# Local attention and a state-space layer: 448 rows cut as 128, 128, 128 and 64, with the 64s of two tokens or steps side by side

## The chip, the cores and the metric

The kernel runs on one core of a Trainium2 chip. The metric is device time in microseconds (us), lower is better. The times of the kernel before are 172.17, 172.98 and 174.47 us, median 172.98. Engines are named as in the profile: PE is TensorE's matmul, PEld its weights load, DVE VectorE, ACT ScalarE, POOL GpSimd, SP SyncE, whose queue issues most transfers.

## The reference, cut to what matters

Two layers stand side by side; the output joins them along the last axis. S = 2048 tokens, D = 448.

```python
# A: sliding, dilated local attention, 16 heads of 28, window 8, dilation 2
qkv = (x @ wqkv).reshape(B, S, 3, H, Dh)
idx = pos[:, None] - 2 * arange(8)          # masked where negative
logits = einsum("bhsd,bhswd->bhsw", q, k[idx]) * Dh ** -0.5
o = einsum("bhsw,bhswd->bhsd", softmax(logits), v[idx])
a = o.reshape(B, S, D) @ wo
# B: diagonal complex state space layer with 448 states
h_t = Lam_bar * h_{t-1} + B_bar @ x_t       # over all 2048 steps
b = 2 * real(C @ h_t) + x * Dskip
out = concatenate([a, b], axis=-1)
```

## The kernel before, in words

All is bf16 with float32 sums. The queue of every engine is written out by hand: what the program says in one order is issued in that order. Only DVE's larger pieces wait in a list (`add`), and `pump` puts them out when the running total of DVE's costs is below that of PE's costs; `pe(...)`, `dve(...)` and `load[0] +=` keep these totals. They are costs written by the author, and they set DVE's order and not PE's.

The 2048 tokens lie on 128 partitions with 16 tokens (`j`) each. The 448 features, wherever they are contracted, are cut in four tiles of `KT` = 112 rows.

- `g_xta` (L299): for a pair of tokens, 8 transposes on PE (L304) and one copy on DVE (L305) give x with features on the rows.
- `proj(t, j)` (L309): q, k or v of one token: 4 matmuls 448 wide (L312), one ACT copy (L316). 48 of them.
- `b_weights` (L323), `b_x` (L332): the state space input weights (8 matmuls, L327), and x transposed for it (L337), copied by DVE for even and ACT for odd steps (L339, L342).
- `c_weights` (L345): 56 small transposes that put 64 columns each in the upper or lower half of a PSUM bank (L352).
- `ssm_in(hf, j)` (L365): for half `hf` of the states (four or three tiles of 128 rows, 64 states with real and imaginary part) and step `j` of 8: 4 matmuls 256 wide for each tile (L372), then, but for step 0, one with the step before (L378), then the ACT copies (L379). The 4 matmuls of a step stand ahead of those that need the step before.
- `scan_mul` (L384), `scan_pe` (L391), `scan_run` (L403), `scan_out` (L410): the recurrence over blocks of 8 steps, by turns on DVE and PE; `ssm_mix` (L415) brings its result to the steps.
- `ssm_out(j, cb)` (L428): the output: 7 matmuls with C (L432), 4 with the diagonal Dskip (L434), an ACT copy, a store.
- `logits`, `softmax` (L448, L481): all on DVE: eight products of 128 x 7168 (L457), sums of halves (L460, L463 and on), and the softmax.
- `pv_mul` (L517): attention times v on DVE (L520); `av(i)` (L526): the sum over the window, done on PE by matmuls with the identity (L537); `wo_j` (L550): the output projection of one token, 4 matmuls 448 wide (L554), a copy, a store.

The order of PE's work: transposes with the k and q projections; v with `b_x` and `b_weights` in between; the rest of q; `ssm_in` of the first half, `c_weights`, `ssm_in` of the second half with the scans in between; `ssm_mix` and `ssm_out`; then 40 steps of `av` with `wo_j` between them. PSUM has 8 banks, given out in turn (`bank`).

Of the kernel before, what the change touches and what calls it, by code (L numbers as in the profile page):

```python
# [14 lines left out]
J = 16  # L15
# [21 lines left out]
def kernel(  # L37
# [41 lines left out]
    BT = big.tile([KT, 4, NT, 128], BF16, tag="BT")  # L79
    xT = big.tile([KT, 4, T, NC], BF16, tag="xT")  # L80
# [3 lines left out]
    dgD = big.tile([KT, 4, KT], BF16, tag="dgD")  # L84
# [5 lines left out]
    wts = wbuf[0:KT].rearrange("p (a k n) -> p a k n", a=3, k=4)  # L90
# [3 lines left out]
    xTA = u3[0:KT].rearrange("p (k j n) -> p k j n", k=4, j=J)  # L94
# [3 lines left out]
    w_r = A_wqkv.rearrange("(k p) n -> p k n", p=KT)  # L98
    xB_r = B_x[0].rearrange("(c p j) d -> p c j d", p=128, j=T)

    def load_w(t):
        SP.dma_start(wts[:, t], w_r[:, :, t * D:(t + 1) * D])
# [6 lines left out]

    load_x(14, 16)  # L110
# [6 lines left out]
    prow = const.tile([3 * NT, 2, HS], BF16, tag="prow")  # L117
    for i, vec in enumerate((B_Lambda_re, B_Lambda_im, B_log_dt)):
        ACT.dma_start(prow[NT * i:NT * (i + 1)], vec.rearrange("(t i) -> t i", i=HS).unsqueeze(1).to_broadcast((NT, 2, HS)))
    drow = const.tile([4, KT], BF16, tag="drow")  # L120
    ACT.dma_start(drow[:], B_Dskip.rearrange("(t i) -> t i", i=KT))
# [76 lines left out]
    def sincos(sin_out, cos_out, y, tmp):  # L198
        V.tensor_scalar(tmp, y, 1.0, MAGIC, ALU.mult, ALU.add)
        V.scalar_tensor_tensor(tmp, tmp, -MAGIC, y, ALU.add, ALU.subtract)  # L200
        ACT.activation(sin_out, tmp, ACTF.Sin, scale=-2 * PI * SHR)
        ACT.activation(tmp, tmp, ACTF.Abs)
        ACT.activation(cos_out, tmp, ACTF.Sin, bias=hpib[:], scale=-2 * PI * SHR)

# [6 lines left out]
    prm = pt_("prm", (128, 3, NT))  # L211
    lre, lim, ld = prm[:, 0], prm[:, 1], prm[:, 2]
    dsk = pt_("dsk", (KT, 4))
# [8 lines left out]
    def params_in():  # L222
        tp = bank(BF16)
        PE.transpose(tp[:, 0:3 * NT], prow.rearrange("p a i -> p (a i)"), ident[0:3 * NT, 0:3 * NT])
        V.tensor_copy(prm.rearrange("p a b -> p (a b)"), tp[:, 0:3 * NT])
        tp = bank(BF16)
        PE.transpose(tp[0:KT, 0:4], drow[:], ident[0:4, 0:4])
        V.tensor_copy(dsk[:], tp[0:KT, 0:4])
        ACT.activation(dt[:], ld, ACTF.Exp)
        dve(0.3)  # L230

    def params1():
# [3 lines left out]
        ACT.activation(rk[:], rk[:], ACTF.Exp)  # L236
# [3 lines left out]
        sincos(sn[:], cs[:], yk[:], tk[:])  # L240
# [3 lines left out]
        V.reciprocal(den[:], den[:])  # L244

# [35 lines left out]
    def build_D():  # L281
        V.tensor_tensor(dgD[:], ident[0:KT, 0:KT].unsqueeze(1).to_broadcast((KT, 4, KT)),
                        dsk.unsqueeze(2).to_broadcast((KT, 4, KT)), ALU.mult)
# [14 lines left out]

    def g_xta(jp):  # L299
        tp = bank(BF16)  # L300
        tpv = tp[0:KT].rearrange("p (k j n) -> p k j n", k=4, j=2)
        for kt in range(4):
            for jj in range(2):
                PE.transpose(tpv[:, kt, jj, :], xnA[:, 2 * jp + jj, KT * kt:KT * (kt + 1)], ident[:])  # L304
        V.tensor_copy(xTA[:, :, 2 * jp:2 * jp + 2, :], tpv)  # L305
        dve(0.69)
        load[0] += 0.45

    def proj(t, j):  # L309
        ps = bank()  # L310
        for kt in range(4):
            PE.matmul(ps[:, 0:D], xTA[:, kt, j, :], wts[:, t, kt, :], start=(kt == 0), stop=(kt == 3))  # L312
        src = ps[:, 0:D].rearrange("p (h d) -> p d h", h=H)
        dst = (q_s[:, :, j * H:(j + 1) * H] if t == 0 else
               k_s[:, :, HALO + j, :] if t == 1 else v_s[:, HALO + j])
        ACT.copy(dst, src)  # L316
        count[2] += 1
        if acts and count[2] > 18 and count[2] % 2 == 0:
            acts.pop(0)()
        pe(0.76)  # L320


    def b_weights(t):  # L323
        ps = bank()
        for kt in range(4):
            for i in range(2):
                PE.matmul(ps[0:KT, 128 * kt:128 * (kt + 1)], Bn[:, t, KT * kt:KT * (kt + 1)], G[:, i, t, :],  # L327
                          start=(kt == 0 and i == 0), stop=(kt == 3 and i == 1))
        ACT.copy(BT[:, :, t, :], ps[0:KT].rearrange("p (k n) -> p k n", k=4))
        pe(0.45)  # L330

    def b_x(j):  # L332
        tp = bank(BF16)
        tpv = tp[0:KT].rearrange("p (k c n) -> p k c n", k=4, c=2)
        for kt in range(4):
            for c in range(2):
                PE.transpose(tpv[:, kt, c, :], xnB[:, c, j, KT * kt:KT * (kt + 1)], ident[:])  # L337
        if j % 2 == 0:
            V.tensor_copy(xT[:, :, j, :], tp[0:KT].rearrange("p (k n) -> p k n", k=4))  # L339
            dve(0.69)  # L340
        else:
            ACT.copy(xT[:, :, j, :], tp[0:KT].rearrange("p (k n) -> p k n", k=4))  # L342
        load[0] += 0.45

    def c_weights(t2):  # L345
        n = min(2, NT - 2 * t2)
        tp = bank(BF16)
        for i in range(n):
            t = 2 * t2 + i
            for ri in range(2):  # L350
                for dt_ in range(4):
# [13 lines left out]
    def ssm_in(hf, j):  # L365
        banks = []
        for pr_ in pairs(halves[hf]):
            ps = bank()
# [157 lines left out]
    def av(i):  # L526
# [3 lines left out]
        if s == 0:  # L530
            accs[n_] = [bank() for _ in range(nj)]
# [175 lines left out]
```

## Time and profile before

| | us |
|---|---|
| median of 3 runs | 172.98 |
| the profiled execution's own time | 172.66 |
| its span | 170.9 |
| PE busy (95% of the span) | 162.5 |
| DVE busy (86%) | 146.7 |
| ACT busy (56%) | 95.7 |
| PE idle from 33 to 71 us | 0.00 |
| PE idle from 71 to 75.6 us | 1.56 |
| PE idle from 98.3 to 126.7 us | 0.00 |
| PE idle from 126.7 to 167.5 us | 0.01 |

The granted TensorE clock is 0.998 over the execution. Busy time counts an engine as busy while at least one instruction is in it. Matmuls overlap in PE, so the mean duration of one is longer than the time that it adds to a run of its kind; that time is read from the starts of the runs in the timeline. A line as `L312 PE MATMUL b<-wbuf,u 112*128 112x448 bf16 x192` says: L312 is line 312 of the listing; PSUM bank `b` is written from the weights `wbuf` and the data `u`; the weights are 112 rows by 128 columns, the streamed data 112 rows by 448, and there are 192 of them. A timeline row has start, duration from the first start to the last end, engine, line, operation and, in square brackets, how long the engine was idle ahead of it and what released it.

### The profile page before, as it was taken

To read this page: it belongs to the slowest core of one execution; us is meant where nothing else is said; L and a number is where in the kernel's file an instruction comes from. 1 tells how busy PE (TensorE), PEld (TensorE's weight loads), DVE (VectorE), ACT (ScalarE), POOL (GpSimd) and SP (SyncE) were. 2 spreads that over 40 slices of the span, in tenths; PEclk is the share of its full clock that TensorE was granted. 3 is DMA by queue.
4 is the path that set the end of the run, shared out by engine and by line. 5 is a ranking of instruction groups with operands and counts; after the bars stand their busy time and mean duration, and the time that the engine had idled before them with its cause. 6 is when DMAs were issued, how large, how long until landed. Compare 5 with 4: busy or idle time off the path is not lost.

```text
span 170.9 us, 3793 instructions
## 1 busy us (share of the span) xinstructions
PE 162.5 (95%) x1584; PEld 120.0 (70%) x1586; DVE 146.7 (86%) x179; ACT 95.7 (56%) x184; POOL 2.8 (2%) x22
## 2 busy tenths in 40 slices
PE   6799999999999999959999899999999999999992
PEld 6565655777756888838886555655679988888870
DVE  1399999899999999999998999989999999656811
ACT  3095569999887355524469954496430527145431
POOL 3000000000000000000010000000000000000000
PEclk9999999999999999999999999999999999999999
DMA  5999990892099000000000002202232010111112
GB/s 164 319 244 208 351 216 22 183 162 37 4 188 186 2 4 0 4 0 0 0 4 0 0 27 70 68 28 80 76 106 80 0 58 30 58 54 56 58 54 81
DMA packets 13279, 14.01 MB, mean 82 GB/s; under 512 B 4543, under 2 KB 12495, under 8 KB 13135
## 3 DMA queue, kind: packets, MB, share of 16 engines
q1 hardware_dynamic: 13191, 13.77, 32.1%
q8 instruction: 12, 0.20, 0.5%
q14 instruction: 5, 0.04, 0.1%
q10 hardware_dynamic: 71, 0.01, 0.0%
HBM read 6.89 MB, written 3.67 MB: 62 GB/s over the span
## 4 chain that ended last, share of the span: by engine, by line
PE 50%; DVE 34%; ACT 6%; issue 4%; DMA 3%; SPq 0%; DVEq 0%; ACTq 0%
PE b L537 17%; PE b L432 12%; DVE u L457 11%; PE b L554 7%; PE b L312 6%; DVE u L460 6%; DVE l L463 3%; DMA u<-in_A_x_dram 3%; PE b L422 2%; PE b L420 2%; DVE R L207 2%; PE b L434 2%; DVE l L466 2%; ACT k_s L316 2%; DVE u L406 1%
## 5 line engine op out<-in xcount | busy, mean ns | idle before, releaser
L312 PE MATMUL b<-wbuf,u 112*128 112x448 bf16 x192 | 40.1, 352 | 0.1
L520 DVE TENSOR_TENSOR k_s<-u,v_s 128x1792 bf16<-128x1792 bf16 (+1 forms) x40 | 33.8, 903 | 6.2 <-PE b L537 6.2
L537 PEld LDWEIGHTS <-k_s 128*112 128x112 bf16 x512 | 30.6, 130 | 2.0
L457 DVE TENSOR_TENSOR u<-q_s,k_s 128x7168 bf16<-128x7168 bf16 x8 | 31.1, 3889 | 0.9 <-ACT tab L294 0.5
L537 PE MATMUL b<-ident,k_s 128*112 128x128 bf16 x512 | 30.9, 219 | 0.0
L312 PEld LDWEIGHTS <-u 112*128 112x128 bf16 x192 | 17.7, 97 | 14.0 <-DVE u L305 0.5
L372 PE MATMUL b<-xT,BT 112*128 112x256 bf16 x224 | 26.9, 272 | 0.1
L379 ACT CAST u<-b 128x512 bf16<-128x512 f32 (+1 forms) x32 | 15.6, 535 | 19.0 <-PE b L378 16.7
L372 PEld LDWEIGHTS <-BT 112*128 112x128 bf16 x224 | 21.7, 97 | 3.3
L432 PE MATMUL b<-Cw,u 128*128 128x448 bf16 x112 | 23.8, 352 | 0.0
L559 ACT CAST ya<-b 128x448 bf16<-128x448 f32 x15 | 8.1, 537 | 16.8 <-PE b L554 13.4
L460 DVE TENSOR_TENSOR u<-u 128x3584 bf16<-128x3584 bf16 x8 | 16.2, 2022 | 0.1
L432 PEld LDWEIGHTS <-u 128*128 128x128 bf16 x112 | 10.5, 98 | 7.5
L436 ACT CAST yo<-b 128x448 bf16<-128x448 f32 x16 | 8.4, 534 | 12.1 <-PE b L434 8.7
L554 PE MATMUL b<-u,q_s 112*128 112x448 bf16 x64 | 14.4, 352 | 0.0
L423 ACT CAST u<-b 128x512 bf16<-128x512 f32 (+1 forms) x28 | 13.1, 561 | 0.4 <-PE b L422 0.4
L547 ACT CAST q_s<-b 112x512 bf16<-112x512 f32 x14 | 7.3, 595 | 8.1 <-PE b L537 8.0
L316 ACT CAST q_s<-b 128x448 bf16<-128x448 f32 x16 | 8.5, 532 | 4.3 <-PE b L312 4.3
L316 ACT CAST k_s<-b 128x448 bf16<-128x448 f32 x16 | 8.0, 533 | 4.2 <-PE b L312 4.2
L422 PE MATMUL b<-u,R 128*128 128x255 bf16 x49 | 9.5, 272 | 0.7 <-ACT u L413 0.7
L420 PE MATMUL b<-u,ident 128*128 128x512 bf16 (+1 forms) x28 | 9.9, 353 | 0.0
L316 ACT CAST v_s<-b 128x448 bf16<-128x448 f32 x16 | 9.2, 612 | 0.8 <-PE b L312 0.8
(119 smaller groups left out, 179.7 us busy)
## 6 DMA issues: line engine op xcount, KB each, us to landing
u<-in_B_x_dram SPq DMA_DIRECT2D x2, 896.0 KB, 14.4
out_dram<-yo SPq DMA_DIRECT2D x16, 112.0 KB, 1.7
out_dram<-ya SPq DMA_DIRECT2D x16, 112.0 KB, 1.7
u<-in_A_x_dram SPq DMA_DIRECT2D x3, 448.0 KB
wbuf<-in_A_wqkv_dram SPq DMA_DIRECT2D x3, 392.0 KB, 7.4
k_s<-k_s SPq DMA_DIRECT2D x1, 784.0 KB
v_s<-v_s SPq DMA_DIRECT2D x1, 784.0 KB, 5.9
k_s<-k_s SPq DMA_DIRECT2D x1, 588.0 KB, 10.6
```

What stands on the lines that cost most here:

```text
L312: PE.matmul(ps[:, 0:D], xTA[:, kt, j, :], wts[:, t, kt, :], start=(kt == 0), stop=(kt == 3))
L316: ACT.copy(dst, src)
L372: PE.matmul(ps[:, i * NC:(i + 1) * NC], BT[:, kt, t, :], xT[:, kt, j, :], start=(kt == 0 and i == 0), stop=(kt == 3 and j == 0 and i == le ...
L379: ACT.copy(Z[:, pr_[0]:pr_[0] + n, j, :], ps[:, 0:n * NC].rearrange("p (t c) -> p t c", t=n))
L420: PE.matmul(ps[:, 0:n * NC], ident[:], Z[:, sl, j, :], start=True, stop=False)
L423: ACT.copy(Z[:, sl, j, :], ps[:, 0:n * NC].rearrange("p (t c) -> p t c", t=n))
L432: PE.matmul(ps[:, 0:D], Z[:, t, j, cols], Cw[:, t, :], start=(t == 0), stop=False)
L457: V.tensor_tensor(pr[:], qv, kv, ALU.mult)
L460: V.tensor_tensor(pr[:, :, 0:14, :], pr[:, :, 0:14, :], pr[:, :, 14:28, :], ALU.add)
L520: V.tensor_tensor(pv_of(i), attn[:, s, H * j0:H * (j0 + nj)].rearrange("p (j h) -> p j h", h=H) .unsqueeze(2).to_broadcast((128, nj, DH, H ...
L537: PE.matmul(acc[kt // kb][0:KT, o:o + 128], pvf[:, jj, KT * kt:KT * (kt + 1)], ident[:], start=(s == 0 and o == 0), stop=(s == W - 1 and o ...
L554: PE.matmul(ps[:, 0:D], oTs[n_ % 3][:, kt, jj, :], wo_p[:, kt, :], start=(kt == 0), stop=(kt == 3))
```

## The change

Wherever 448 rows are contracted, the four tiles of 112 become three of 128 and a rest of 64. Two rests, of two tokens or two steps, lie on rows 0 to 63 and 64 to 127 of the same tile, and their products are issued one after the other, each on its half of the array's rows and into a bank of its own (`pair_product`, `sums_half`). Where a 64 wide result is transposed or summed, two go to columns 0 to 63 and 64 to 127 of the array and to the two halves of a bank's partitions (`transposes`, `b_weights`, `av`). For that, projections and output projection work on pairs of tokens, and `ssm_in` becomes a generator that puts the input sums of two steps out ahead of the steps that use them. `ssm_out` has three products 128 wide and one 64 wide, alone on half of the rows, for the skip.

Moved along with it: the weights' last 64 rows are loaded twice, once for each half of the partitions, by transfers of their own (two on ACT's queue at the start, two on SP's); the parameters gain Dskip, and are transposed after the first projection pair; the exponent and the sines of the parameters get a place of their own (`params_act`); `c_weights` goes to and fro between the halves; one logits buffer gets memory of its own; `oTs` has two buffers where it had three; DVE's list is pumped at a few more places, and the first `scan_mul` comes after five of DVE's eight logits products where it came after six.

```diff
-    xT = big.tile([KT, 4, T, NC], BF16, tag="xT")
+    xT = big.tile([128, T // 2, 7, NC], BF16, tag="xT")
...
     def load_w(t):
-        SP.dma_start(wts[:, t], w_r[:, :, t * D:(t + 1) * D])
+        SP.dma_start(wts[:, t, 0:3], w_r[:, :, t * D:(t + 1) * D])
+
+    def load_wh(eng, ts):
+        for i in range(2):
+            eng.dma_start(wts[HS * i:HS * (i + 1), ts, 3], wh_r[:, ts])
...
+    load_wh(ACT, slice(1, 2))
+    prow = const.tile([4 * NT, 2, HS], BF16, tag="prow")
+    for i, vec in enumerate((B_Lambda_re, B_Lambda_im, B_log_dt, B_Dskip)):
+        ACT.dma_start(prow[NT * i:NT * (i + 1)], vec.rearrange("(t i) -> t i", i=HS).unsqueeze(1).to_broadcast((NT, 2, HS)))
     load_x(14, 16)
     load_w(1)
...
+    load_wh(SP, slice(0, 3, 2))
     load_w(2)
...
+    def transposes(tp, x_of):
+        for kt in range(3):
+            for jj in range(2):
+                PE.transpose(tp[:, (2 * kt + jj) * 128:(2 * kt + jj + 1) * 128], x_of(jj, 128 * kt, 128 * (kt + 1)), ident[:])
+        for jj in range(2):
+            PE.transpose(tp[HS * jj:HS * (jj + 1), 768:896], x_of(jj, 384, 448), ident[:])
...
-    def proj(t, j):
-        ps = bank()
-        for kt in range(4):
-            PE.matmul(ps[:, 0:D], xTA[:, kt, j, :], wts[:, t, kt, :], start=(kt == 0), stop=(kt == 3))
+    def pair_product(lhs_of, rhs_of, rhs_half):
+        ps = [bank(), bank()]
+        for jj in range(2):
+            for kt in range(3):
+                PE.matmul(ps[jj][:, 0:D], lhs_of(jj, kt), rhs_of(kt), start=(kt == 0), stop=False)
+        for jj in range(2):
+            rows = slice(HS * jj, HS * (jj + 1))
+            PE.matmul(ps[jj][:, 0:D], lhs_of(jj, 3), rhs_half[rows], start=False, stop=True)
+        return ps
+
+    def proj(t, jp):
+        def lhs(jj, kt):
+            return xTA[:, jp, 2 * kt + jj, :] if kt < 3 else xTA[HS * jj:HS * (jj + 1), jp, 6, :]
+        ps2 = pair_product(lhs, lambda kt: wts[:, t, kt, :], wts[:, t, 3, :])
+        for jj in (1, 0):
...
+            ACT.copy(dst, src)
...
     def b_weights(t):
         ps = bank()
-        for kt in range(4):
+        for kt in range(3):
             for i in range(2):
-                PE.matmul(ps[0:KT, 128 * kt:128 * (kt + 1)], Bn[:, t, KT * kt:KT * (kt + 1)], G[:, i, t, :],
-                          start=(kt == 0 and i == 0), stop=(kt == 3 and i == 1))
+                PE.matmul(ps[:, 128 * kt:128 * (kt + 1)], Bn[:, t, 128 * kt:128 * (kt + 1)], G[:, i, t, :],
+                          start=(kt == 0 and i == 0), stop=False)
+        for i in range(2):
+            for a in range(2):
+                PE.matmul(ps[HS * a:HS * (a + 1), 384:512], Bn[:, t, 384:448], G[:, i, t, :],
+                          start=False, stop=(i == 1))
...
+    def b_x(jp, c):
         tp = bank(BF16)
+        transposes(tp, lambda jj, lo, hi: xnB[:, c, 2 * jp + jj, lo:hi])
+        o = xT[:, jp, :, 128 * c:128 * (c + 1)]
+        src = tp[:, 0:896].rearrange("p (k n) -> p k n", k=7)
+        if c == 0:
+            V.tensor_copy(o, src)
...
+            ACT.copy(o, src)
...
+    def sums_full(hf, j):
+        sums[hf, j] = [(bank(), pr_) for pr_ in pairs(halves[hf])]
+        jp, jj = j // 2, j % 2
+        for ps, pr_ in sums[hf, j]:
             for i, t in enumerate(pr_):
+                for kt in range(3):
+                    PE.matmul(ps[:, i * NC:(i + 1) * NC], BT[:, t, kt, :], xT[:, jp, 2 * kt + jj, :],
+                              start=(kt == 0 and i == 0), stop=False)
...
+    def sums_half(hf, jp):
+        for b_, pr_ in enumerate(pairs(halves[hf])):
+            for i, t in enumerate(pr_):
+                for jj in range(2):
+                    rows = slice(HS * jj, HS * (jj + 1))
+                    PE.matmul(sums[hf, 2 * jp + jj][b_][0][:, i * NC:(i + 1) * NC], BT[rows, t, 3, :], xT[rows, jp, 6, :],
+                              start=False, stop=(jp == 0 and jj == 0 and i == len(pr_) - 1))
...
+    def ssm_in(hf):
+        sums_full(hf, 0)
+        sums_full(hf, 1)
+        sums_half(hf, 0)
+        yield
+        for jp in range(T // 2):
+            ssm_step(hf, 2 * jp)
+            if jp + 1 < T // 2:
+                sums_full(hf, 2 * jp + 2)
+            yield
+            ssm_step(hf, 2 * jp + 1)
+            if jp + 1 < T // 2:
+                sums_full(hf, 2 * jp + 3)
+                sums_half(hf, jp + 1)
+            yield
...
-        for kt in range(4):
-            PE.matmul(ps[:, KT * kt:KT * (kt + 1)], xT[:, kt, j, cols], dgD[:, kt, :], start=False, stop=(kt == 3))
+        jp, jj = j // 2, j % 2
+        for kt in range(3):
+            PE.matmul(ps[:, 128 * kt:128 * (kt + 1)], xT[:, jp, 2 * kt + jj, cols], dgD[:, 128 * kt:128 * (kt + 1)],
+                      start=False, stop=False)
+        rows = slice(HS * jj, HS * (jj + 1))
+        PE.matmul(ps[:, 384:448], xT[rows, jp, 6, cols], dgD[rows, 384:448], start=False, stop=True)
...
     def av(i):
...
+        todo_ = [(jj, kt) for kt in range(4) for jj in range(nj)]
...
+        for key in todo_:
+            jj, kt = key
+            b_, rows, o = place[key]
+            PE.matmul(acc[b_][rows, o:o + 128], pvf[:, jj, 128 * kt:min(D, 128 * (kt + 1))], ident[:],
...
-    def wo_j(n_, jj):
+    def wo_pair(n_, jp):
...
+        ps2 = pair_product(lhs, lambda kt: wo_p[:, kt, :], wo_p[:, 3, :])
...
     g_xta(7)
+    g_xta(6)
+    proj(1, 7)
     params_in()
...
+    g_xta(5)
+    params1()
+    proj(1, 6)
+    params_act()
...
-    for j in range(15, -1, -1):
-        proj(2, j)
-        if j % 2 == 1:
-            b_x(7 - j // 2)
-        elif j > 0:
-            b_weights(j // 2 - 1)
+    for jp in range(7, -1, -1):
+        proj(2, jp)
+        b_x((7 - jp) // 2, jp % 2)
+        if jp > 0:
+            b_weights(jp - 1)
...
+    second = ssm_in(1)
+    next(second)
+    pump(2.0)
     banks = scan_pe(0, 1)
     scan_run(banks)
     scan_mul(0)
-    for j in range(1, 6):
-        ssm_in(1, j)
+    for _ in range(6):
+        next(second)
     banks = scan_pe(0, 0)
     scan_out(banks)
-    ssm_in(1, 6)
-    ssm_in(1, 7)
+    for _ in second:
+        pass
```

`ssm_step(hf, j)` is the second half of the old `ssm_in`: the products with the step before, and the copies. The place of a rest in `av` is, for token `jj` of a group, the upper half of the partitions where `jj` is even and the lower where it is odd.

## The prediction

> **What bounds the kernel now.** I read the page's head first (busy shares and slices), then the chain, then stages in the timeline, then the groups of PE by shape, and last single instructions around the one place where the kernel already puts two half-width products side by side.
>
> ```profile
> span 170.9 us, 3793 instructions
> PE 162.5 (95%) x1584; PEld 120.0 (70%) x1586; DVE 146.7 (86%) x179; ACT 95.7 (56%) x184; POOL 2.8 (2%) x22
> PE   6799999999999999959999899999999999999992
> DVE  1399999899999999999998999989999999656811
> PE 50%; DVE 34%; ACT 6%; issue 4%; DMA 3%; SPq 0%; DVEq 0%; ACTq 0%
> ```
>
> PE is near full in every slice but 19, DVE nearly so until slice 34. The list of waits says how little PE is held:
>
> ```profile
> PE b L397 <- DVE wbuf L387: 1.6, 1, 1.6
> PE b L398 <- DVE wbuf L388: 0.2, 1, 0.2
> PE b L422 <- ACT u L413: 0.7, 1, 0.7
> ```
>
> The chain runs through DVE from 33 to 92 us, since DVE is full there too; PE has no wait in that stretch, and what either queue gains the other caps. So PE is the bound from 7 us to 167.5 us, with 1.8 us lent to DVE at 75 us and 0.7 us to ACT at 98 us. What PE streams sets the time. Timeline rows give the price of one product in a run of its kind (start to start; the "mean ns" of a matmul holds its pipeline too and is no price):
>
> ```profile
> 135.52 0.92 PE L554 MATMUL b<-u,q_s 112*128 112x448 bf16 x4
> 136.28 1.95 PE L537 MATMUL b<-ident,k_s 128*112 128x128 bf16 x32
> 99.60 0.36 PE L434 MATMUL b<-dgD,xT 112*128 112x112 bf16 x4
> ```
>
> Four products 448 wide take 136.28 - 135.52 = 0.76, so 0.189 each; 32 products 128 wide run from 136.28 to 138.07, so 0.056 each; four 112 wide take 0.20 (99.60 to 99.80), so 0.050. A product 256 wide is 0.109 (the sixteen L372 and four L378 from 57.80 to 59.99: 20 in 2.19).
>
> Before, L352 (c_weights) already writes 64 columns of the array, first the upper then the lower half:
>
> ```profile
> 70.81 0.27 PE L378 MATMUL b<-u,R 128*128 128x256 bf16 x1
> 71.01 0.24 PEld L352 LDWEIGHTS <-u 112*64 112x64 bf16 x7 [0.21 <-issue]
> 71.01 0.35 PE L352 MATMUL b<-ident,u 112*64 112x112 bf16 x6
> ...
> L352 PE MATMUL b<-ident,u x56: 212/213/237, 71.0 to 72.4; 112*64 112x112 bf16 x56
> ...
> 72.39 0.21 PE L352 MATMUL b<-ident,u 112*64 112x112 bf16 x1
> 72.54 0.28 PE L372 MATMUL b<-xT,BT 112*128 112x256 bf16 x1
> ```
>
> Two things are to be seen. The 56 products start within 1.38 us, 0.025 each, half of 0.050: two halves do run at once. And each change between the whole array and halves costs: the last L378 has streamed at 70.81 + 0.11 = 70.92, yet neither weights nor product follow until 71.01 (elsewhere the next weights load begins with the product ahead of them); the last L352 ends its 0.05 at 72.44, and the next product starts at 72.54. From 70.92 to 72.54 are 1.62 us; 28 pairs at 0.050 are 1.40. **One visit to halves costs 0.22 us.**
>
> **The change part by part.** It cuts 448 into 128, 128, 128, 64 and pairs the 64s.
>
> *What PE saves in streams.* Projections: 24 pairs of tokens, 8 products become 6 and one pair, -0.189 each; output: 8 pairs the same; together 32 x 0.189 = -6.0. Sums over the state inputs: four visits in the first half of the states (8 products of 0.109 in 4 slots, -0.436) and four in the second (6 in 3, -0.327): -3.1. av: 24 steps of 16 products become 14 slots (-0.112), 16 steps of 8 become 7 (-0.056): -3.6. Transposes (g_xta, b_x): 16 x -0.056 = -0.9. b_weights: 8 slots stay 8. ssm_out: 3 x 0.056 + about 0.03 for the 64 wide rest against 4 x 0.050: nothing. c_weights only changes order, and it ran in pairs already: nothing. Sum -13.6.
>
> *What PE pays in visits.* In PE's order each projection pair, output pair, sums_half, av step, group of transposes, b_weights and ssm_out goes to halves once and comes back: 24 + 8 + 8 + 40 + 16 + 7 + 16 = 119. At 0.22: +26.2. The lower end for a visit to halves of the columns (63 of them: 16 transposes, 7 b_weights, 40 av) is the two gaps alone, 0.09 + 0.10 = 0.19; the upper is 0.25, with the start of the second tile 0.03 behind. For halves of the rows (56: projections, output, sums, ssm_out) no row shows both edges. Two rows bound it: a product with fewer rows but full columns that costs nothing, L312's 112 rows after L304's 128, and the parameters' transpose with 21 rows:
>
> ```profile
> 5.61 0.42 PE L304 MATMUL b<-ident,u 128*112 128x128 bf16 x2
> 5.96 0.20 PE L224 MATMUL b<-ident,prow 21*128 21x21 bf16 x1
> ```
>
> The second L304 starts near 5.71 and streams 0.107 at the pace of that stretch (eight in 4.97 to 5.82); L224 follows 0.14 later, though its data had long landed: SP's transfer that waits for the same semaphore was issued before 3.1 us. That is nearer to the column visits than to nothing, so I take 0.22 for rows too, and keep 0 and 0.25 as ends.
>
> On packing, the trace's gap of 0.22 us per visit is what counts. [...]
>
> *The chain between steps.* ssm_in had each step's input sums ahead of its R products, covering ACT's copy of the step before. Now step 6 and step 7 of each half stand with nothing between. After step 6's products of bank one (0.22) come about 0.20 to ACT's start and 0.58 of copy (L379): PE waits about 0.6, and 0.25 more for bank two: 0.85. In the second half scan_out's two copies (0.53 each) stand ahead on ACT: about 1.6. Together +2.4.
>
> *DVE's queue.* Order: the first scan product (scan_mul) now comes after five logits products, not six, so 3.89 + 2.02 + 1.09 = 7.0 us earlier. That frees PE's 1.8 us at 75 us: -1.8. It needs that slack: the parameters' transpose moves behind the first projection pair (9.5 instead of 6 us), its exponent waits on ACT behind two copies, and params2, R, params3, G and tables (11 us of DVE work) shift with it, so the first logits product moves from 25.2 to near 29; later xT copies wait for PE up to 3 us, as b_x gives DVE the second of each pair of groups, not the first. 3.5 + 3 is within 7.0 only just. Later the debt returns: after the last scan product DVE has 26.1 us (95.45 to 121.55) to the first attention product, now 26.1 + 3.89 + 1.09 + 2.35 = 33.4; with the product 34.5. PE reaches av 31.2 us after it (126.7), plus 16 visits in ssm_out, 34.7. A tie; DVE's 1.0 us a step is av's too (0.90 - 0.11 + 0.22). I put 0 on it, up to 3 if it slips.
>
> *Loads and ends.* Two half loads of 57 KB on ACT's queue stand ahead of the parameters', SP gets two for the other weights and one more for wo. Bytes ahead of the second x load grow by 58 KB, at the 350 GB/s of that stretch +0.2; the fourth and fifth x loads wait for those half loads; PE needs them only after the first pair, so I put nothing on it. At the end both tokens of the last pair finish together and their two stores queue on SP: +0.3. The output buffers oTs go from three to two, which costs nothing: group n's copies come a whole group after the products that read group n - 2.
>
> **Sum.** -13.6 + 26.2 + 2.4 - 1.8 + 0.5 = +13.7. The profiled execution took 172.66 (1.8 beside its span), 0.3 below the median of the runs: 172.66 + 13.7 = 186.4.
>
> **Rivals.**
> 1. *Rows switch for nothing, columns do not.* 63 visits x 0.22 = 13.9; -13.6 + 13.9 + 1.1 = +1.4, 174.1: no change. For it: no row shows the way back. Against: L224's gap.
> 2. *Halves of the rows do not run at once.* Streams saved shrink by 6.0 + 3.1: 195.5. For it: only column halves are seen side by side. Against: the two write different banks, as L352's halves write different partitions.
> 3. *No visit costs anything* (the gaps at 71 us belong to that one place): faster. PE saves 13.6, but DVE then sets the end: its first attention product near 123, eight steps at 1.0 to 131, then PE's 16 x 0.78 + 16 x 0.39 + 8 x 1.32 = 29.3, and 3.4 of end: span 164, 166. The sign turns where a visit costs (13.6 - 1.1) / 119 = 0.105 us, half of what is measured.
>
> **How the numbers follow.** Forecast 0.73; by its own bounds (119 visits at 0.19 to 0.25, the waits between steps 0 to 2.4, DVE's debt 0 to 3) 180 to 193. Rival 1: 0.09. Rival 2: 0.08. Rival 3: 0.06. Something else, 0.04, likelier slower. The range reaches down to rival 1's time and up to just short of rival 2's, 174 to 195, and leaves out rival 3, most of rival 2 and the ends of the rest. About 2% is what a measurement of this kernel can tell. Faster is rival 3: 0.06. Same is rival 1: 0.09. Slower is the rest, 0.85.
>
> **What would show it.** In the profile after: an av step of 16 products at about 1.0 us against 0.90; a gap near 0.09 us ahead of and behind every 64-wide group; a projection pair near 1.55 against 1.51; ssm_out near 1.74 against 1.52; no PE wait on the first scan product; a PE wait on ACT's copy of a state step near the end of each ssm_in. I am wrong if pairs take 1.32 and av steps 0.78, or if PE waits long on DVE ahead of the first av.

## The result and the profile after

The changed kernel takes 187.55 us (median of 4 runs, 186.71 to 187.84); the kernel before, run on the same chip beside it, 173.72 us (172.17 to 176.05). The ratio is 1.082 with a 95% interval of [1.072, 1.092]: slower, and 13.8 us by the medians. The profiled execution took 187.84 us, 1.7 beside its span, and is 15.2 us above the profiled execution of before; the stages below are counted against that 15.2. In experiments 1 and 5, in the first two joined versions below and beside them some runs were disturbed; the medians and ranges given hold them, the ratios leave them out.

The head of the page of the changed kernel, as above for the kernel before:

```profile
span 186.1 us, 3823 instructions
PE 175.5 (94%) x1597; PEld 109.7 (59%) x1599; DVE 146.3 (79%) x182; ACT 93.7 (50%) x184; POOL 2.8 (2%) x22
PE   7999999999999998899798999999599999999991
DVE  1369999793999997799599999959999999441811
PEclk9999999999999999999999999999969999999999
PE 89%; DVE 5%; ACT 3%; issue 1%; POOL 0%; DVEq 0%; ACTq 0%; POOLq 0%
```

DVE has as much to do as before (146.3 us), but it is no longer full between slices 3 and 34, where 7, 3, three more 7s, 5 and 5 stand among the nines. PE carries 89% of the chain instead of 50%. Slice 30 of the granted clock (PEclk) reads 6: something new.

Where PE's time went is read from single rows of the timeline: a projection pair, the sums, ssm_out, and an output pair between av steps. A slot below is the time of one product in a run of its kind, as the prediction took it (0.189 us for 448 columns, 0.109 for 256, 0.056 for 128); a visit is the way to halves of the array and back.

```profile
52.37 1.31 PE L326 MATMUL b<-wbuf,u 128*128 128x448 bf16 x6
53.61 0.36 PE L329 MATMUL b<-wbuf,u 64*128 64x448 bf16 x2
53.91 1.31 PE L326 MATMUL b<-wbuf,u 128*128 128x448 bf16 x6
...
59.70 0.61 PE L412 MATMUL b<-xT,BT 64*128 64x256 bf16 x8
60.25 1.48 PE L402 MATMUL b<-xT,BT 128*128 128x256 bf16 x12
...
100.31 1.49 PE L492 MATMUL b<-Cw,u 128*128 128x448 bf16 x7
...
120.88 1.49 PE L492 MATMUL b<-Cw,u 128*128 128x448 bf16 x7
122.20 0.33 PE L495 MATMUL b<-dgD,xT 128*128 128x128 bf16 x3
122.46 0.20 PE L498 MATMUL b<-dgD,xT 64*128 64x64 bf16 x1
122.59 1.50 PE L492 MATMUL b<-Cw,u 128*128 128x448 bf16 x7
...
147.83 1.31 PE L326 MATMUL b<-u,q_s 128*128 128x448 bf16 x6
149.07 0.36 PE L329 MATMUL b<-u,q_s 64*128 64x448 bf16 x2
149.37 4.10 PE L620 MATMUL b<-ident,k_s 128*128 128x128 bf16 x64
153.40 1.31 PE L326 MATMUL b<-u,q_s 128*128 128x448 bf16 x6
```

A projection pair lasts from 52.37 to 53.91, 1.54. Seven slots of 0.189 are 1.32, so the visit costs 0.22. Its two edges can be seen: six whole products from 52.37 end at 53.50, the halves begin at 53.61; they take one slot between them, to 53.80, and the next whole product begins at 53.91. Both halves do run at once, and 0.11 goes by on either side. The load of their weights is not brought forward either: it starts with them, at 53.61, while the load for the last whole product starts at 53.14, one product ahead of it. Eight halves of the sums end 0.11 before 60.25 in the same way (59.70 + 4 x 0.109 = 60.14). ssm_out takes 1.71 (120.88 to 122.59), against 1.52. Four av steps take 4.03 (149.37 to 153.40), 1.01 each, against 0.90 before.

The list of waits has an entry that was not there and one that is nearly gone:

```profile
DVE xT L367 <- PE b L312: 4.4, 2, 3.1
DVE wbuf L447 <- ACT u L422: 3.8, 2, 2.3
PE b L620 <- DVE k_s L584: 2.3, 1, 2.3
PE b L421 <- ACT u L422: 1.4, 2, 0.9
...
PE b L457 <- ACT u L422: 0.6, 1, 0.6
```

At the first scan's products PE waits 0.6 us, and no longer 1.6 and 0.2, and for ACT instead of DVE; but it waits 2.3 us for DVE's first attention product. Behind that wait PE is slow for a while; here are its stretches (length, then busy time and, in brackets, instructions of PE, PEld, DVE, ACT and POOL, then the granted clock, the DMA share and GB/s):

```profile
131.97:134.29 2.32, 0.00 (x1) 0.01 (x1) 2.29 (x3) 0.53 (x1) 0.00 (x0) 1.00 0.20 66
134.29:135.40 1.11, 1.11 (x17) 0.87 (x18) 1.11 (x2) 0.00 (x0) 0.00 (x0) 0.90 0.38 100
135.40:138.00 2.60, 2.60 (x27) 2.23 (x26) 2.60 (x3) 0.00 (x0) 0.00 (x0) 0.50 0.37 113
```

In the third of them the clock is 0.50 and a product takes about twice its time. Read in stretches of half a microsecond, the slow time lasts 3.4 us, from 135.2 to 138.6. Twelve av steps from 134.29 take 13.5 us, where 12 x 1.01 are 12.1.

The difference by stages of PE's timeline, profiled execution against profiled execution (us):

| stage | before | after | difference |
|---|---|---|---|
| start of the span to the first projection | 7.6 | 6.6 | -1.0 |
| first projection to the sums (projections, transposes, b_weights) | 46.3 | 50.4 | +4.1 |
| sums, steps, scans | 44.4 | 43.3 | -1.1 |
| ssm_out with the last mixes | 28.3 | 31.7 | +3.4 |
| PE waits for DVE ahead of av | 0 | 2.3 | +2.3 |
| av and output products | 40.9 | 47.9 | +7.0 |
| last product to the end | 3.4 | 3.9 | +0.5 |

### The profile page after: what moved, and what is told of

It reads as the page before. It is cut to its first block, busy times and chain, and to the rows that moved or that the text cites. A ratio compares the mean times of both kernels' runs of the same rounds, so it can differ in the third digit from the quotient of the medians.

```text
span 186.1 us, 3823 instructions
## 1 busy us (share of the span) xinstructions
PE 175.5 (94%) x1597; PEld 109.7 (59%) x1599; DVE 146.3 (79%) x182; ACT 93.7 (50%) x184; POOL 2.8 (2%) x22
## 4 chain that ended last, share of the span: by engine, by line
PE 89%; DVE 5%; ACT 3%; issue 1%; POOL 0%; DVEq 0%; ACTq 0%; POOLq 0%
PE b L326 21%; PE b L620 19%; PE b L402 10%; PE b L492 9%; PE b L329 5%; PE b L310 4%; PE b L421 3%; PE b L480 3%; PE b L482 3%; PE b L412 2%; PE b L141 2%; PE b L352 2%; PE b L312 1%; ACT u L422 1%; PE b L495 1%
## 5 line engine op out<-in xcount | busy, mean ns | idle before, releaser
L620 PE MATMUL b<-ident,k_s 128*128 128x128 bf16 (+1 forms) x512 | 36.0, 229 | 2.3 <-DVE k_s L584 2.3
L620 PEld LDWEIGHTS <-k_s 128*128 128x128 bf16 (+1 forms) x512 | 27.8, 103 | 10.8 <-DVE k_s L584 2.8
L326 PE MATMUL b<-wbuf,u 128*128 128x448 bf16 x144 | 31.4, 354 | 0.1
L402 PE MATMUL b<-xT,BT 128*128 128x256 bf16 x168 | 20.7, 273 | 0.1
L326 PEld LDWEIGHTS <-u 128*128 128x128 bf16 x144 | 12.1, 98 | 11.9 <-issue 1.8
L402 PEld LDWEIGHTS <-BT 128*128 128x128 bf16 x168 | 16.2, 98 | 2.6 <-issue 0.4
L630 ACT CAST q_s<-b 128x512 bf16<-128x512 f32 (+1 forms) x14 | 6.7, 552 | 20.2 <-PE b L620 20.2
L648 ACT CAST ya<-b 128x448 bf16<-128x448 f32 x15 | 7.3, 535 | 16.1 <-issue 12.1
L492 PEld LDWEIGHTS <-u 128*128 128x128 bf16 x112 | 10.2, 98 | 7.8
L326 PE MATMUL b<-u,q_s 128*128 128x448 bf16 x48 | 10.5, 354 | 0.0
L341 ACT CAST v_s<-b 128x448 bf16<-128x448 f32 x16 | 8.1, 586 | 3.0 <-PE b L329 3.0
## 6 DMA issues: line engine op xcount, KB each, us to landing
u<-in_B_x_dram SPq DMA_DIRECT2D x2, 896.0 KB, 13.8
```

What stands on the lines that cost most here:

```text
L326: PE.matmul(ps[jj][:, 0:D], lhs_of(jj, kt), rhs_of(kt), start=(kt == 0), stop=False)
L402: PE.matmul(ps[:, i * NC:(i + 1) * NC], BT[:, t, kt, :], xT[:, jp, 2 * kt + jj, :], start=(kt == 0 and i == 0), stop=False)
L492: PE.matmul(ps[:, 0:D], Z[:, t, j, cols], Cw[:, t, :], start=(t == 0), stop=False)
L620: PE.matmul(acc[b_][rows, o:o + 128], pvf[:, jj, 128 * kt:min(D, 128 * (kt + 1))], ident[:], start=(s == 0 and first[b_, rows.start] == ke ...
```

## The experiments

The theory is the one of the prediction: the streams saved are saved, and each visit to halves costs about 0.21 us. Rivals are that only one kind of halves pays, that the half products themselves are dear, and that the moved order and its waits, not the halves, made the kernel slow. The kernel before was run beside each group; its medians there were 172.3 to 173.5 us. All kernels are edits of the changed kernel.

**1. Rows whole.** Where two halves of rows stood, one whole product:

```diff
-for jj in range(2):
-    rows = slice(HS * jj, HS * (jj + 1))
-    PE.matmul(ps[jj][:, 0:D], lhs_of(jj, 3), rhs_half[rows], ...)
+for jj in range(1):
+    PE.matmul(ps[jj][:, 0:D], lhs_of(jj, 3), rhs_half, ...)
```

and in the same way in sums_half and ssm_out.

> In the changed kernel each pair of row halves (projections, output products, input sums, ssm_out's rest) becomes one whole-array product; the halves of columns stay. Left out: the rest of each second token and of each odd step; ssm_out adds the other token's rest too. The order, the loads and the number of stream slots stay as in the changed kernel; 56 visits to row halves are gone, 48 of them ahead of av. Theory (a visit to row halves costs 0.20 to 0.22 us): PE gains 11 to 12 us, of which DVE's debt ahead of av gives some back, since its first attention product cannot come as much earlier: 176 to 179 us. Rival 1 (rows switch for nothing, columns pay all): 187 us, unchanged. Rival (the moved order and its waits made the kernel slower): 185 or more.

Measured: 178.25 us (176.18 to 179.06), ratio to before 1.037 [1.029, 1.046]. The projections, the start of ssm_out, and PE ahead of av:

```profile
50.59 1.30 PE L326 MATMUL b<-wbuf,u 128*128 128x448 bf16 x6
51.73 0.35 PE L329 MATMUL b<-wbuf,u 128*128 128x448 bf16 x1
51.91 2.78 PE L402 MATMUL b<-xT,BT 128*128 128x256 bf16 x24
...
93.64 1.49 PE L492 MATMUL b<-Cw,u 128*128 128x448 bf16 x7
...
125.65 12.17 PE L620 MATMUL b<-ident,k_s 128*128 128x128 bf16 x192 [3.60 <-DVE k_s L584]
```

The pair takes 1.32, seven slots and nothing more, where it took 1.54. ssm_out begins 6.7 us earlier (93.64 against 100.31), 0.21 for each of the 32 visits ahead of it. Rows are not free; and since one product takes a slot where the pair took a slot and 0.22, the two halves had run at once. PE then waits 3.6 us for DVE instead of 2.3: DVE could follow only in part.

**2. Columns whole.** The same for transposes, b_weights and av:

```diff
-place[jj, 3] = (o // 512, slice(HS * (jj % 2), HS * (jj % 2 + 1)), o % 512)
+place[jj, 3] = (o // 512, slice(0, 128), o % 512)
-todo_ = [(jj, kt) for kt in range(4) for jj in range(nj)]
+todo_ = [(jj, kt) for kt in range(4) for jj in range(nj) if kt < 3 or jj % 2 == 0]
```

> In the changed kernel each pair of column halves (transposes, b_weights, av) becomes one whole-array product; the halves of rows stay. Left out: the rest of each second token in the transposes and in av; in b_weights the tile of the rest is written once instead of twice over. Order, loads and stream slots stay; 63 visits to column halves are gone, 40 of them in av. Theory (0.216 us for each visit): av steps of four tokens take 0.79 instead of 1.01 us on PE, PE gains 13.6 us, but DVE's attention products at 1.09 us for four tokens then hold av back and its debt ahead of av stays: 174 to 178 us. Rival (columns switch for nothing, rows pay all): 187 us.

Measured: 175.99 us (175.50 to 176.73), ratio 1.023 [1.016, 1.030]. ssm_out begins 4.7 us earlier (95.58 against 100.31), 0.21 for each of 23 visits. Columns and rows cost the same. In ssm_out and av:

```profile
95.58 1.49 PE L492 MATMUL b<-Cw,u 128*128 128x448 bf16 x7
...
129.55 10.64 PE L620 MATMUL b<-ident,k_s 128*128 128x128 bf16 x148 [2.32 <-DVE k_s L584]
...
142.89 3.30 PE L620 MATMUL b<-ident,k_s 128*128 128x128 bf16 x56
```

Late in av four steps of 14 products take 3.1 us or so, 0.79 each; but in the first stretch a product takes 0.072 (10.64 / 148), for there DVE's attention products, not PE, give the pace (from 129.5 to 136 us DVE is busy for all 6.5 us, PE for 6.2). So part of the 40 visits' 8.6 us is not to be had until DVE is ahead.

**3. Every half a whole product.** No visits, no streams saved, the changed order:

```diff
-PE.matmul(ps[jj][:, 0:D], lhs_of(jj, 3), rhs_half[rows], ...)
+PE.matmul(ps[jj][:, 0:D], lhs_of(jj, 3), rhs_half, ...)
```

and likewise elsewhere, with both halves kept.

> In the changed kernel each half becomes a whole-array product of its own, so that none of the 119 visits is left and no stream is saved against the kernel before, in the changed order. The text that is computed differs: the rests are summed over 128 rows that hold both tokens' rests, or written from columns 320 to 447. Theory (visits less streams saved made the time): 187.5 - 25 + 13.6 = 176 us, less what the slow stretch of PE at av no longer costs: 173 to 177 us, the kernel before within 2%. Rival (the changed order, its waits and DVE's debt are what costs): 184 us or more. Rival (halves do not run at once): 187 - 25 = 163 us, since then no stream would come back.

Measured: 178.46 us (177.05 to 178.89), ratio 1.036 [1.027, 1.044]. That is 1.5 above the theory's range, and nowhere near the rivals' 184 and 163. Why it is not within 2% of before is in one row:

```profile
129.49 10.70 PE L620 MATMUL b<-ident,k_s 128*128 128x128 bf16 x169 [3.60 <-DVE k_s L584]
```

PE reaches av at 125.9 us, 0.7 before it did in the kernel before, and waits 3.6 us for DVE. So the changed order, with the planner's costs as they stood, has a price of its own: DVE comes late to av (DVE's debt). The changed kernel pays 2.3 us of it. The theory had left it out; experiment 6 says where it comes from.

**4. PE kept busy in its wait.**

```diff
+fill = bank()
+for _ in range(40):
+    PE.matmul(fill[:, 0:128], ident[:], ident[:], start=True, stop=True)
 for i, (n_, s) in enumerate(steps):
```

> The changed kernel with 40 products of the identity with itself between ssm_out and the first av product (40 x 0.056 = 2.2 us), where PE waits 2.3 us for DVE; nothing is left out. Theory (the stretch from 135.4 to 138 us in which PE's products take 0.107 us each comes of that wait): the granted clock stays at 1.00 there, twelve av steps take about 12.1 instead of 13.6 us, total 186.0 to 186.6 us. Rival (the stretch comes of something else at that place, such as the load of the output weights at 109 GB/s): the slow stretch stays, 187.5 to 188 us.

Measured: 186.70 us (186.26 to 186.92), ratio 1.084 [1.078, 1.091]: 0.85 less than the changed kernel, though work was added; the two ratios to the kernel before (1.084 and 1.082) do not tell them apart, the rows do. The stretch behind the wait:

```profile
134.30:138.00 3.70, 3.70 (x61) 3.03 (x60) 3.70 (x5) 0.00 (x0) 0.00 (x0) 1.00 0.40 114
```

61 products in 3.7 us, at a clock of 1.00, while the load of the output weights still runs at 114 GB/s. The twelve av steps take 12.1 us, as expected, instead of 13.5. All four runs had clocks of 0.996 to 1.000; three of four runs of the changed kernel had 0.989 to 0.991, and its one run at 0.998 took 186.71. The load is not what makes the slow stretch: it runs here at full clock, and the slow stretch of the second joined version below has no transfer beside it (0 GB/s). That the idle time makes it is likely, but a wait of the same 2.32 us was followed by none in the profiled executions of experiments 2, 7 and 11, so filling the gap was not proved to be what kept the clock up here.

**5. More visits, the same products.**

```diff
-todo_ = [(jj, kt) for kt in range(4) for jj in range(nj)]
+todo_ = [(jj, kt) for j0 in range(0, nj, 2) for kt in range(4) for jj in (j0, j0 + 1)]
```

> The changed kernel with one order changed in av: a step of four tokens goes to halves twice, after the whole tiles of tokens 0 and 1 and after those of 2 and 3, instead of once. The same products, 24 visits more; nothing is left out. Theory (each visit costs 0.21 to 0.22 us by itself, whatever is done in it): +5.2 us on PE, which is the bound there, 192.7 us, an av step of four tokens 1.22 us. Rival (what costs is the half products, not the going to and fro): unchanged, 187.5 us.

Measured: 194.41 us (192.39 to 195.89), ratio 1.114 [1.103, 1.124]; the profiled run took 193.05 us, 5.2 more than that of the changed kernel.

```profile
151.88 5.01 PE L620 MATMUL b<-ident,k_s 128*128 128x128 bf16 x64
156.83 1.31 PE L326 MATMUL b<-u,q_s 128*128 128x448 bf16 x6
```

The 64 products that took 4.03 take 4.95: 0.23 for each of four visits more. The half products are the same ones; what costs is to go there and come back.

**6. The planner's costs.** The planner sets how much of DVE's work is put ahead of each piece of PE's; its costs had not been told of the visits.

```diff
-pe(1.35)            # projection and output pairs
+pe(1.54)
-load[0] += 0.42     # transposes
+load[0] += 0.6
```

and so on for five more.

> The changed kernel with the planner's costs of PE's work set to what the trace shows (projection pair 1.54 for 1.35, transposes 0.60 for 0.42, b_weights 0.70 for 0.50, sums_half 0.20 more, ssm_out 1.73 for 1.53, av 1.00 for 0.80); PE's order is the same, DVE's logits move ahead of the copies and of the first scan product. Nothing is left out. Theory (DVE's debt ahead of av comes of its 8 us of waits for PE and ACT at 45 and 75 us, which come of costs that left out the visits): PE's wait of 2.3 us ahead of av and the slow stretch behind it go, PE may wait for the first scan product for up to 1.8 us as before: 183 to 185.5 us. Rival (the debt is DVE's work itself): 187 to 188 us.

Measured: 184.04 us (183.76 to 184.20), ratio 1.063 [1.057, 1.070]. PE's order is unchanged; its waits and DVE's:

```profile
DVE k_s L584 <- PE b L620: 14.2, 12, 3.4
...
PE b L421 <- ACT u L422: 1.4, 2, 0.9
...
PE b L457 <- DVE Cw L382: 0.6, 1, 0.6
```

PE no longer waits ahead of av; DVE is ahead and waits for PE there (14.2 us in 12 places). The debt was made of DVE's idle time in the changed kernel: 1.3, 3.1, 1.5, 1.1 and 2.3 us at 34, 45, 75, 79 and 92 us, and 2.1 us at 126 us, where the softmax waits for ACT. With the new costs 0.4 and 0.9 us are left of it, at 92 us and in the softmax, and DVE begins its attention products 10.9 us earlier (122.3 against 133.2). So the idle time came of costs which put too little work ahead of it. 3.5 us of the 13.8, the slow stretch among them, are the planner's and not the halves'.

**7. av without halves, streams saved.** 448 + 448 = 7 x 128: two tokens' rows lie one behind the other, so seven whole tiles cover both. The fourth holds the even token's last 64 rows and the odd token's first 64. The output product of the odd token takes a second copy of the weights, shifted by 64 rows.

```diff
+for m in range(nm):                       # nm = 7 * nj // 2
+    b_, o = m // 4, 128 * (m % 4)
+    PE.matmul(acc[b_][:, o:o + 128], pvf[:, 128 * m:128 * (m + 1)], ident[:], ...)
...
+SP.dma_start(wo_p[HS:128, 3, :], wo_r[0:4])
+for kt in range(3):
+    SP.dma_start(wo_p[:, 4 + kt, :], wo_r[8 * kt + 4:8 * kt + 12])
```

> The changed kernel, with av's 896 rows of two tokens cut into seven whole tiles of 128, the fourth of which holds the rest of the even token and the first 64 rows of the odd one; the output product of the odd token takes its weights from a second copy that is shifted by 64 rows. Nothing is left out; av needs no halves. Theory (40 visits at 0.216 us gone, streams saved kept): -8.6 us on PE, of which DVE's attention products at 1.09 us for four tokens give some back: 179 to 181.5 us. Rival (the visits of av are hidden or cost nothing): 187.5 us.

Measured: 180.37 us (180.35 to 180.66), ratio 1.043 [1.036, 1.049].

```profile
147.98 3.30 PE L601 MATMUL b<-ident,k_s 128*128 128x128 bf16 x56
151.12 1.30 PE L326 MATMUL b<-u,q_s 128*128 128x448 bf16 x6
```

Four steps in 3.14, 0.785 each, 14 slots of 0.056 and nothing beside them, with the whole result computed. Not all of the 7.2 us below the changed kernel is visits: PE waits 2.3 us for DVE here too, but no slow stretch follows, which is about 1.4 us; and the first twelve steps take 11.8 us, at DVE's pace, so that their visits bring almost nothing.

**8 to 10. Joined throughout, and DVE's queue.** The first joined version does the same for the projections' transposes, gives ssm_out's rest a whole product against a table with zeros, takes two pairs of projections into one visit, and puts other work between steps 6 and 7; 45 visits are left of 119.

```diff
-PE.matmul(ps[:, 384:448], xT[rows, jp, 6, cols], dgD[rows, 384:448], ...)
+PE.matmul(ps[:, 384:448], xT[:, jp, 6, cols], dgD[:, 384 + HS * jj:384 + HS * (jj + 1)], ...)
-for jp in (3, 2, 1, 0):
-    proj(0, jp)
+proj(0, 3, 2)
+proj(0, 1, 0)
```

> As the last one, and the projections' transposes cut in the same way (seven whole tiles for two tokens, a second copy of the weights shifted by 64 rows); ssm_out's rest as one whole product against a table with zeros for the other step; two pairs of projections share a visit; two groups of c_weights stand between steps 6 and 7 of the first half of the states, scan_pe between those of the second; the planner's costs are as measured. Nothing is left out. Theory: 40 + 8 + 16 + 10 visits at 0.21 gone (-15.5), the wait and the slow stretch at av gone (-3.8), cover -1.4: PE would end at 167; DVE's first attention product, with logits from 27 us on and no idle time, comes near 123.5 us, which gives about the same end: 166 to 171 us, faster than the kernel before. Rival (DVE's debt is the bound once PE is fast): 173 us or more.

Measured: 173.63 us (172.57 to 176.06), ratio 1.003 [0.998, 1.009]. The expectation (166 to 171) failed by 2.6 us, and the waits say where:

```profile
PE b L466 <- DVE wbuf L456: 4.6, 2, 2.9
DVE wbuf L456 <- ACT u L431: 4.4, 1, 4.4
```

At the two scans the engines wait for each other: PE behind a logits product of 3.9 us that DVE had just begun, DVE idle where nothing had been put ahead. The next version moves two more steps ahead of the first scan product, more logits ahead of the second half's, and b_x's copies to ACT.

```diff
-next(second)
+for _ in range(3):
+    next(second)
...
-pump(2.0)
+pump(5.0)
 scan_mul(1)
```

> As the last but with DVE's queue mended where the trace of that run shows it and PE waiting for each other: two more steps of the second half of the states stand ahead of the first scan product (PE waited 2.9 us there), more logits ahead of the second half's scan products (DVE idle 4.4 us, PE waiting 1.7 us there), and ACT, not DVE, copies all of b_x's transposes (2.5 us off DVE). Nothing is left out. Theory (PE's products set the time once neither of the two waits): 5 us of PE's waits and part of the slow stretches behind them go, DVE's first attention product comes 6 to 7 us earlier: 166 to 169 us, faster than the kernel before by 2 to 4%. Rival (ACT or PSUM's banks hold the v projections, with 2.5 us more on ACT there): 171 us or more.

Measured: 172.40 us (170.61 to 174.00), ratio 0.997 [0.993, 1.001]. The expectation failed again. PE waits for ACT nowhere in the v projections (the rival's cause); its longest wait is now at one place, and the clock halves behind it:

```profile
90.50:93.10 2.60, 0.07 (x1) 0.00 (x0) 2.56 (x4) 1.61 (x4) 0.00 (x0) 1.00 0.00 0
93.10:96.60 3.50, 3.49 (x12) 1.65 (x12) 2.79 (x6) 0.85 (x2) 0.00 (x0) 0.52 0.00 0
```

The 5.0 had put one logits half (2.0 us) too much ahead.

```diff
-pump(5.0)
+pump(3.0)
 scan_mul(1)
...
-pump(2.0)
 banks = scan_pe(1, 1)
```

> As the last but one (the version with joined rests and mended queue), with one logits half less ahead of the second half's first scan product and none ahead of its scan; nothing is left out. There PE waited 2.5 us for that product at 93 us, and its products ran at half pace from 94 to 96.5 us. Theory: DVE's product then comes 2 us earlier, PE's wait falls to 0.6 us or less and the slow stretch (1.7 us) goes with it: 168 to 169.5 us, faster than the kernel before by 2%. Rival (DVE's work is the bound, so that a PE that waits less there waits more ahead of av): 171 to 172.5 us.

Measured: 168.88 us (168.63 to 169.16), ratio 0.979 [0.975, 0.984]: faster than both kernels, than the one before by 2.1% (1.6 to 2.5). Its page:

```profile
span 167.3 us, 3690 instructions
PE   6689999999999999997998989999999999999991
DVE  1267999999999999999999999999999999965711
PEclk9999999999999999999999999999999999999999
```

DVE is full again to slice 35, and the clock is whole. Streams saved and visits left give -13.6 + 45 x 0.21 = -4.2 on PE; the total is 3.5 us lower.

**11. Cover between steps 6 and 7**, in the changed kernel:

```diff
-for _ in ssm_in(0):
-    pass
+first = ssm_in(0)
+for _ in range(8):
+    next(first)
+c_weights(0)
+c_weights(1)
+for _ in first:
+    pass
```

> The changed kernel with two groups of c_weights between steps 6 and 7 of the first half of the states, and scan_pe's second products between those of the second half; nothing is left out. Theory (PE's waits for ACT's copies of step 6, 0.46 and 0.95 us, come of nothing standing between the two steps): these waits go, but PE then only waits longer for DVE ahead of av (2.3 us becomes 3 to 3.7), so that the total stays within 0.5 us of 187.5 us. Rival (they set the end): 186.1 us.

Measured: 187.89 us (187.85 to 187.91), ratio 1.091 [1.088, 1.094]. Nothing is gained, as the theory said, but the time goes elsewhere than it said:

```profile
71.94 0.61 PE L421 MATMUL b<-u,R 128*128 128x256 bf16 x4
72.48 0.98 PE L380 MATMUL b<-ident,u 112*64 112x112 bf16 x32
73.39 0.61 PE L421 MATMUL b<-u,R 128*128 128x256 bf16 x4
...
78.84 0.39 PE L457 MATMUL b<-wbuf,ident 128*128 128x512 bf16 x1 [1.62 <-DVE wbuf L447]
```

Steps 6 and 7 have no wait between them any more, and PE waits 1.62 us for the first scan product instead; the wait ahead of av stays at 2.3. The slow stretch has moved too: it now lies behind the wait at 78.8 us (nine products of the sums from 80.22 take 2.13 us, where nine alike take 1.15 in the changed kernel, and the slice of the clock from 79.1 to 83.7 us reads 6), and none follows the wait ahead of av (clock 1.00 from 135.7 to 142). So PE comes to av 1.5 us later than in the changed kernel and leaves the first twelve steps at the same time (147.85 against 147.83).

## Why the prediction was right, point by point

- *Streams saved (-13.6).* Held. Both kinds of halves run at once: a pair takes one slot, as the rows of the projections show and experiment 1 confirms. Rival 2 falls. (The slice in which PE was not full before is the eighteenth, not 19; nothing rests on it.)
- *119 visits at 0.22 (+26.2).* Held: rows 0.21 (experiment 1), columns 0.21 (experiment 2), 0.23 where visits were added (experiment 5); about +25. The choice of 0.22 for rows was right, but it was made by one gap of 0.14 us ahead of a transpose of 21 rows, in a stretch where a product took 0.107 us instead of 0.056; so weak a ground makes it luck in part. Rival 1 falls in experiment 1 by 9 us, rival 3 with every row. Two halves share one slot (eight halves of the sums from 59.70 to 60.25: four slots of 0.109 and one edge of 0.11), and a visit costs its two edges of 0.11 us, at neither of which the weights are loaded a product ahead (loads at 53.61 and 53.90, their products at 53.61 and 53.91). No run tells apart what an edge consists of.
- *Waits between steps 6 and 7 (+2.4).* Mechanism right, size 2.0. In the first half step 6 ends at 72.68, step 7's products start at 73.31 and take 0.25 longer: 0.88, against 0.85. In the second the gap is 1.1, against 1.6; I had put scan_out's copies further into the wait than they reach.
- *First scan product (-1.8).* -1.2: the wait of 1.8 became one of 0.6, which the profile puts down to ACT, just then copying the second half's step 0 (from 78.10 us). DVE had its product's place in the queue early enough: it stood idle for 1.5 us until ACT had copied step 7, and began it at 74.83, where it had begun at 74.85.
- *Loads (+0.2).* Wrong in sign: the first projection starts 1.0 us earlier. The second group of transposes came at 5.83 us, where it had come at 7.1; which of the moved loads did it was not tried.
- *First logits product near 29.* It came at 26.8. The shift of 3.8 us that I had summed was 1.6; 1.0 of the difference is the earlier start, the rest was not traced.
- *DVE's debt (0, up to 3).* 2.3, inside the bound but not at the value I took. The waits for xT came as forecast (4.4 in all, 3.1 at 45 us). What I had not followed is that they come from the planner's costs (experiment 6), and that this same idle time would be the debt. Here one of the prediction's own signs of being wrong came true, a long wait of PE for DVE ahead of the first av; it is the longest wait that PE has in this kernel.
- *Tail (+0.3).* +0.5.
- *Not in the sum:* the slow stretch behind that wait, about +1.5 in the profiled execution.
- *The signs asked for.* An av step takes 1.01 (1.0 was named), a projection pair 1.54 (1.55), ssm_out 1.71 (1.74), the gaps 0.11 (0.09); PE waits for ACT near the end of each ssm_in. The wait at the first scan product, which was to go, is 0.6.

With the sizes measured: -13.6 + 25.2 + 2.0 - 1.2 - 1.0 + 0.5 + 2.3 + 1.5 = 15.7, against 15.2 between the profiled executions. The forecast of +13.7 was thus near for two reasons: the large terms were right to 1 us, and, by luck, the start (1.2 better) made up for part of the debt and its slow stretch (3.8 worse).

## What to carry to other kernels

Count visits, not half products: with 0.21 us for each way in and out, a pair of halves that saves one product of 0.056 us loses, one that saves 0.189 about breaks even (0.02 short), and several pairs in one visit win (four pairs of the sums save 0.436 for one visit). Before halving, look whether two rests fill a whole tile (448 + 448 = 7 x 128 here), with the operand on the other side shifted to fit. And when PE's pieces change their length, the costs by which another engine's work is put ahead must change with them, or that engine idles first and is waited for later, as DVE in the changed kernel: idle for 11.4 us in six places, then waited for 2.3 us.

## What the runs showed of the hardware that was not expected

Two pairs in one visit cost no more than one. In the second joined version twelve whole products and four halves of the projections:

```profile
13.58 2.43 PE L333 MATMUL b<-wbuf,u 128*128 128x448 bf16 x12
15.95 0.55 PE L337 MATMUL b<-wbuf,u 64*128 64x448 bf16 x4
16.43 0.56 PE L321 MATMUL b<-ident,u 128*128 128x128 bf16 x7
```

From 13.58 to 16.43 are 2.85; fourteen slots of 0.189 are 2.65, which leaves 0.20 for the visit.

PE's granted clock fell behind waits of PE in five of the profiled executions: the changed kernel (wait 2.3 us), experiment 5 (2.3), the first joined version (2.9), the second (2.5) and experiment 11 (1.6); one of the page's 40 slices of the clock reads 6 behind each of these waits. In the changed kernel the clock was 0.50 for 3.4 us, from 0.9 us after PE had started again; in the second joined version it was 0.52 over the 3.5 us from 93.1; in the first joined version and in experiment 11 nine products 256 wide of the sums took 2.13 us from the first start to the last end behind the wait (from 79.59 and from 80.22), where nine alike take 1.15 in the changed kernel (from 79.60). The slow time cost 1.4 us in the changed kernel and 1.7 us in the second joined version, beside the wait. The length of the wait does not decide it: in experiments 1 and 3 PE waited 3.6 us ahead of av, in 2, 7 and 11 it waited 2.3 us there, and behind these waits the clock of the profiled executions stayed at 1.00. The mean clock goes with the spread of runs that are otherwise alike: of the kernel before, 31 runs with a mean clock of 0.996 or more have a median of 172.1 us, 16 with 0.987 to 0.990 one of 174.1. What decides it was not settled.
